# Hedgehog attention with a gated MLP: two heads' output rows moved into spare rows, and another order of loads and stores in the output stage

## The chip, the cores and the metric

The kernel runs on one core of a Trainium2 chip. A core has five engines that work side by side: TensorE (PE, matrix products, with its weight loads shown as PEld), VectorE (DVE), ScalarE (ACT), GpSimd (POOL) and SyncE (SP), which here does little but issue DMAs. The metric is the device time in microseconds (us) of one execution; the number compared is the median of several executions. The kernel before takes 686.28 us (three runs, 686.24 to 686.62).

## The reference

With S = 2048 tokens, D = 640, 32 heads of 20 columns, F = 1536, all in float32:

```python
qkv = (x @ wqkv)                      # split in q, k, v and 32 heads
pq, pk = q @ w_phi, k @ w_phi         # per head, 20 x 20
phi_q = concat(softmax(pq), softmax(-pq))   # 40 features a head
phi_k = concat(softmax(pk), softmax(-pk))
kv, z = phi_k^T @ v, sum_s phi_k      # per head, 40 x 20 and 40
o = (phi_q @ kv) / (phi_q . z + 1e-6)
s = o @ wo                            # heads side by side, 640 x 640
g = silu(gelu(xn @ w1 + b1) @ w2 + b2)
out = x + s * g                       # xn = layernorm(x) feeds both branches
```

## The kernel before, in words

The kernel has three stages. The first (0 to about 270 us) normalises x, projects keys, values and queries, and sums `kv` and `z` over all tokens. The second (to about 580 us) is the MLP, in twelve units; beside it the query features are normalised tile by tile (`q_norm`, 128 tokens a tile) and written to a DRAM array `phi_dram`. The third is the output stage, to which nearly all of the change belongs.

Matrix products keep float32 accuracy by splitting each operand in a high and a low part (type `F32R`) and adding three products: high times high, high times low, low times high (`PASSES`).

**The output stage.** Tokens are handled in four chunks of 512 (`ORDER` = chunks 2, 3, 0, 1; the loop index is `ci`), each in five *blocks* `d`, one for each 128 output columns. A block is one pass of the inner loop:

- `load_res` loads the residual x (`xres`) and, for the first two chunks, the gate (`gt`) of the block two further on;
- `finish(c, d, ...)` multiplies the chunk's attention output `oT` with `wo` in 16 matmuls, multiplies with the gate (VectorE), adds the residual (GpSimd) and stores 256 KB;
- `num_groups` takes a quarter of the work on the next chunk's attention output. There are twelve steps `(j, p)`: `j` is a group of six heads (j = 5 the last two heads, 30 and 31) and `p` a half of the chunk (two tiles of 128 tokens). `num_t` transposes the features `phi` of a step on TensorE and copies them to `ph`; a block later `num_m` multiplies them with the block-diagonal `bdk` (or `bdl` for j = 5), and ScalarE and VectorE write the result's high and low part into `oT`;
- `late_q` carries on the normalisation of the last four query tiles (4 to 7): `q_load` loads one (`eq`, 640 KB), GpSimd and VectorE work on it, and it is stored to `phi_dram`. This runs through the first chunk and the first two blocks of the second.

An attention output of six heads has 120 rows; `bdk` spaces it to 2 x 64 rows, so that 8 of the 128 rows of each of the five `oT` tiles are zero, and `wo` is laid out to match (680 rows). The last two heads' 40 rows stand three times in a tile of their own, `oTl` (high, low and high part), and the sixteenth matmul of `finish` multiplies it with `wol`, which `load_wol` prepares (40 rows of `wo` three times).

`load_phi(c)` issues the loads of a chunk's four `phi` tiles (640 KB each) together: for the third chunk in block 0 of `ci` 0, for the fourth in block 3 of `ci` 1.

**What sets the order.** Everything here stands under `manual_schedule`, so each engine executes its instructions in the order in which the Python code issues them. SP issues every load and store of this stage, in that same order; an instruction that waits holds all that SP has behind it. Tiles come from pools of fixed size (`slabs` 23, `rows` 11, `late` 13); a tile that is asked for when all are taken waits until an older one is read for the last time.

Of the kernel before, what the change touches and what calls it, by code (L numbers as in the profile page):

```python
# [45 lines left out]
def hedgehog_gated_mlp_kernel(ctx: ExitStack, tc: tile.TileContext, x, xt_in, wqk, bd, wv, wo, w1, b1, w2, b2, out_t):  # L46
# [62 lines left out]
    for h in range(3):  # L109
# [4 lines left out]
    lowsel = const.tile([P, 1], F32, name="lowsel")  # L114
    nc.gpsimd.memset(lowsel[:], -1.0)
    nc.gpsimd.affine_select(out=lowsel[:], in_=lowsel[:], pattern=[[0, 1]],
                            compare_op=OP.is_ge, fill=0.0, base=-80, channel_multiplier=1)
    midsel = const.tile([P, 1], F32, name="midsel")
    nc.gpsimd.memset(midsel[:], -1.0)
    nc.gpsimd.affine_select(out=midsel[:], in_=midsel[:], pattern=[[0, 1]],  # L120
                            compare_op=OP.is_ge, fill=0.0, base=-40, channel_multiplier=1)
    nc.gpsimd.affine_select(out=midsel[:], in_=midsel[:], pattern=[[0, 1]],
                            compare_op=OP.is_ge, fill=0.0, base=79, channel_multiplier=-1)
    const.tile([P, 8], F32, name="align")
    bdk = const.tile([P, 10, 64], F32, name="bdk")
    bdl = const.tile([P, 120], F32, name="bdl")
# [436 lines left out]
    def kv_rest():  # L563
        kv_acc(NT - 1, phis.pop(NT - 1), vs.pop(NT - 1))
        kvr = const.tile([P, 360], F32, name="kvr")
        nc.gpsimd.memset(kvr[64:96, 320:360], 0.0)
        nc.gpsimd.memset(kvr[96:, 240:360], 0.0)
        for p, a, b in ((P, 0, 240), (96, 240, 320), (64, 320, 360)):
            nc.scalar.activation(kvr[:p, a:b], kvp[0][:p, a:b], AF.Copy)
        return kvr  # L570


    def kv_state(kvr):
        nc.gpsimd.memset(bdk[:, :, 60:], 0.0)
# [4 lines left out]
        nc.vector.tensor_tensor(bdk[:120, :, :60].rearrange("p f (h d) -> p f h d", d=20),  # L579
                                s3[:, :, None, :20].to_broadcast([120, 10, 3, 20]),  # L580
                                mask[:120, None, :, None].to_broadcast([120, 10, 3, 20]), op=OP.mult)
        for r in range(3):
            nc.vector.tensor_tensor(bdl[:80, 40 * r:40 * r + 40].rearrange("p (h d) -> p h d", d=20),
                                    ps[:80, None, 320:340].to_broadcast([80, 2, 20]),
                                    mask[:80, :2, None].to_broadcast([80, 2, 20]), op=OP.mult)
# [95 lines left out]

    def q_load(t):
        e = slab(F32, "eq")
        ef = e[:].rearrange("p a b -> p (a b)")
        nc.sync.dma_start(ef, e_dram[t])
        return ef

    def q_norm(t, ef):
        ez = slab(F32, "ez")
        zv = ez[:].rearrange("p a b -> p (a b)")  # L690
        nc.gpsimd.tensor_tensor(zv, ef, zf, op=OP.mult)  # L691
# [12 lines left out]
        nc.vector.tensor_tensor(r3, r3, den[:, :, None].to_broadcast([P, 32, 2]), op=OP.mult)  # L704
        yield
        scale_heads(ef, rc)
        yield
        nc.sync.dma_start(phi_dram[t], ef)

    def load_wol():  # L710
        raw = row([P, D], F32, "raw")
        for r in range(3):
            nc.sync.dma_start(raw[40 * r:40 * r + 40, :], wo[640:680, :])
        wol_h = row([P, D], F32R, "wolh")
        wol = row([P, D], F32R, "wol")
        nc.vector.tensor_copy(wol_h[:120, :], raw[:120, :])
        nc.vector.scalar_tensor_tensor(wol[:120, :], wol_h[:120, :].bitcast(F32), midsel[:120, :], raw[:120, :],
                                       op0=OP.mult, op1=OP.add)
        return wol


    def load_phi(c):
        tl = [slab(F32R, "phi", (P, 2 * D)) for _ in range(TPC)]
        for i in range(TPC):
            nc.sync.dma_start(tl[i][:].bitcast(F32), phi_dram[TPC * c + i])
        return tl
# [14 lines left out]
    def num_m(j, oT, p, n, ph):  # L741
# [9 lines left out]
        else:  # L751
            for a, b in ((0, 64), (64, 120)):
                nc.tensor.matmul(po[a:b, :256], bdl[:n, a:b], ph[:n, :256], start=True, stop=True)  # L753
            o2 = oT[1]
            nc.scalar.activation(o2[:120, 0, sl], po[:120, :256], AF.Copy)
            nc.vector.scalar_tensor_tensor(o2[:120, 1, sl], o2[:120, 0, sl].bitcast(F32), lowsel[:120, :],
                                           po[:120, :256], op0=OP.mult, op1=OP.add)

    def num_groups(phi, oT, size=4):
        steps = [(j, p) for p in range(2) for j in range(6)]  # L760
        before = []
        for k in range(0, 12, size):
            now = [(j, p, *num_t(phi, p, j)) for j, p in steps[k:k + size]]
            for j, p, n, ph in before:
                num_m(j, oT, p, n, ph)
            before = now
            yield
        for j, p, n, ph in before:
            num_m(j, oT, p, n, ph)
# [29 lines left out]
    def finish(c, d, oT, last):  # L799
        ps = bankB()  # L800
        steps = [(wo_s[j][:, b, d * P:(d + 1) * P], oT[0][j][:, a, :]) for j in range(5) for a, b in PASSES]
        steps.append((wol[:120, d * P:(d + 1) * P], oT[1][:120, 1, :]))
        for n, (w, o) in enumerate(steps):
            nc.tensor.matmul(ps[:], w, o, start=n == 0, stop=n == 15)  # L804
        xr, gt = xres.pop((c, d)), gates.pop((c, d))
        for o in range(2):
            sl = slice(o * W2, (o + 1) * W2)
# [3 lines left out]
            if last:  # L811
                nc.sync.dma_start(out_t[d * P:(d + 1) * P, c * CW + o * W2:c * CW + (o + 1) * W2], xr[:, sl])
        if not last:
            nc.sync.dma_start(out_t[d * P:(d + 1) * P, c * CW:(c + 1) * CW], xr[:])
# [138 lines left out]
    wol = load_wol()  # L953
# [28 lines left out]
    lq = late_q()  # L982
    for ci, c in enumerate(ORDER):
        nxt = iter(())
# [3 lines left out]
        for d in range(KC):  # L988
            load_res(ci * KC + d + 2)
# [14 lines left out]
def _layout(A_x, A_wqkv, A_w_phi, A_wo, B_w1, B_b1, B_w2, B_b2):  # L1004
# [5 lines left out]
    wo = np.zeros((680, D), a["wo"].dtype)  # L1010
    for k in range(10):
        wo[64 * k:64 * k + 60] = a["wo"][60 * k:60 * k + 60]
    wo[640:] = a["wo"][600:]
# [37 lines left out]
```

## Time and profile before

| what | value |
|---|---|
| median of three runs | 686.28 us (686.24 to 686.62) |
| the profiled execution | 688.63 us |
| its span, first to last instruction | 686.9 us |
| PE busy | 676.7 us (99%), 4713 matmul records |
| DVE, ACT, POOL busy | 455.5, 251.3, 375.6 us |
| L804 (`finish`) with `oT` and `wo` | 300 records, 72.9 us |
| L804 with `oTl` and `wol` | 20 records |
| DMA | 125.73 MB, mean 183 GB/s |

Times in a row are counted from the span's start. A row of the timeline has the start, the length (of all merged instructions), the engine, the line of the kernel, the operation, the tiles (written <- read), the shape and the count. A matmul's own length (about 390 ns) is that of its way through the pipeline; how long one holds TensorE is seen from the distance of two starts. A row of windows has the stretch, the busy time of PE, PEld, DVE, ACT and POOL in it (with counts), the granted TensorE clock, the DMA engines' busy share and GB/s.

### The profile page before, as it was taken

The page shows a single profiled execution, that of the slowest core. Times are in us where ns is not written, and L with a number is a line of the kernel's source. Part 1 is how long each engine was busy: PE and PEld are TensorE (multiplying, and loading weights), DVE is VectorE, ACT ScalarE, POOL GpSimd, SP SyncE. Part 2 cuts the span into 40 slices and gives each one's busy share as a digit, 9 for nine tenths or more (in the row PEclk, how much of TensorE's full clock was granted, in tenths as well). Part 3 has the DMA queues.
Part 4 walks back from the last instruction along what each step waited for, and adds up shares of the span by engine and source line. Part 5 has one row for each costly group of instructions (what it writes and reads, how often), then busy time and mean ns, then how long its engine had stood idle before and what let it go on. Part 6 is the DMA issues. An engine that isn't in the chain of part 4 may idle for free.

```text
span 686.9 us, 11941 instructions
## 1 busy us (share of the span) xinstructions
PE 676.7 (99%) x4713; PEld 590.6 (86%) x4713; DVE 455.5 (66%) x730; ACT 251.3 (37%) x398; POOL 375.6 (55%) x336
## 2 busy tenths in 40 slices
PE   8899999999999999999999999999999999999997
PEld 8899999999999998888887888888888887777875
DVE  4788566886876456677978774676977655774232
ACT  3332313323332237244353347633233354425430
POOL 1355244859577355866968853636456640783221
PEclk9999999999999999999999999999999999999999
DMA  9820052734261153329687697376364491886623
GB/s 339 305 88 2 3 150 81 242 79 149 51 216 59 80 171 134 115 70 329 211 301 260 210 421 319 90 266 240 140 206 153 145 396 49 314 295 210 231 93 107
DMA packets 73966, 125.73 MB, mean 183 GB/s; under 512 B 5694, under 2 KB 42558, under 8 KB 73014
## 3 DMA queue, kind: packets, MB, share of 16 engines
q1 hardware_dynamic: 71606, 114.48, 48.9%
q10 hardware_dynamic: 2304, 10.49, 4.2%
q8 instruction: 37, 0.61, 0.4%
q14 instruction: 19, 0.16, 0.1%
HBM read 79.85 MB, written 45.10 MB: 182 GB/s over the span
## 4 chain that ended last, share of the span: by engine, by line
PE 90%; DVE 5%; ACT 1%; issue 1%; DMA 1%; POOL 1%; SPq 0%; DVEq 0%; POOLq 0%; ACTq 0%
PE pA L306 30%; PE pB L645 22%; PE pB L616 18%; PE pB L804 11%; PE pB L746 3%; PE pB L735 2%; PE kv L377 2%; PE pA L163 2%; DVE y L654 2%; DVE xhi L670 1%; DMA xt<-in_x_dram 1%; PE pA L292 1%; PE pB L753 1%; DVE rc L340 0%; PE pB L590 0%
## 5 line engine op out<-in xcount | busy, mean ns | idle before, releaser
L645 PE MATMUL pB<-hs,w2s 128*128 128x512 f32 x720 | 167.1, 390 | 0.0
L645 PEld LDWEIGHTS pB<-hs,w2s 128*128 128x128 f32 x720 | 134.7, 188 | 29.2 <-PE pB L746 0.8
L616 PE MATMUL pB<-xp,w1s 128*128 128x512 f32 x324 | 81.4, 390 | 1.0 <-DVE pB L888 1.0
L616 PE MATMUL pB<-xd,w1s 128*128 128x512 f32 x324 | 79.3, 389 | 0.0
L332 ACT ACTIVATE e<-e 128x1280 f32<-128x1280 f32 x32 | 40.7, 1272 | 91.5 <-POOL e L327 91.0
L804 PE MATMUL pB<-oT,wo 128*128 128x512 f32 x300 | 72.9, 394 | 0.0
L616 PEld LDWEIGHTS pB<-xp,w1s 128*128 128x128 f32 x324 | 60.7, 188 | 13.9 <-DVE pB L888 1.4
L654 DVE TENSOR_TENSOR y<-pB,y 128x512 f32<-128x512 f32 x100 | 63.9, 680 | 12.3 <-PE pB L645 12.1
L616 PEld LDWEIGHTS pB<-xd,w1s 128*128 128x128 f32 x324 | 60.8, 188 | 12.6
L804 PEld LDWEIGHTS pB<-oT,wo 128*128 128x128 f32 x300 | 55.4, 188 | 14.8 <-ACT ph L738 1.2
L345 POOL TENSOR_TENSOR e<-e,rc 128x1280 f32<-128x1280 f32 x16 | 39.0, 2440 | 48.5 <-DVE rc L365 48.2
L345 POOL TENSOR_TENSOR eq<-eq,rc 128x1280 f32<-128x1280 f32 x16 | 38.0, 2372 | 50.0 <-DVE rc L704 50.0
L327 POOL TENSOR_TENSOR e<-nr,e 128x640 f32<-128x640 f32 x32 | 45.4, 1421 | 33.5 <-DVE nr L326 30.7
L306 PE MATMUL pA<-wv,xp 128*128 128x320 f32 x384 | 61.0, 312 | 0.8 <-DVE nr L326 0.4
L621 ACT ACTIVATE pB<-pB,b1t 128x512 f32<-128x512 f32 x48 | 31.8, 662 | 77.3 <-DVE pB L888 28.4
L306 PE MATMUL pA<-wk,xp 128*128 128x320 f32 x384 | 59.9, 311 | 0.0
L306 PE MATMUL pA<-wq,xp 128*128 128x320 f32 x384 | 59.0, 309 | 0.0
L306 PEld LDWEIGHTS pA<-wv,xp 128*128 128x128 f32 x384 | 56.9, 188 | 1.7 <-issue 0.7
L306 PEld LDWEIGHTS pA<-wq,xp 128*128 128x128 f32 x384 | 56.9, 188 | 0.1
L306 PEld LDWEIGHTS pA<-wk,xp 128*128 128x128 f32 x384 | 56.8, 188 | 0.1
L691 POOL TENSOR_TENSOR ez<-eq,zrep 128x1280 f32<-128x1280 f32 x16 | 47.3, 2953 | 1.1 <-PE pB L753 1.1
L401 POOL TENSOR_TENSOR w1s<-raw,w1s 128x640 fp32r<-128x640 f32 (+1 forms) x18 | 25.7, 1429 | 36.8 <-ACT w1s L400 29.6
(139 smaller groups left out, 1046.0 us busy)
## 6 DMA issues: line engine op xcount, KB each, us to landing
raw<-in_w_dram SPq DMA_DIRECT2D x42, 320.0 KB, 4.4
e_dram<-e ACTq DMA_DIRECT2D x16, 640.0 KB, 3.3
eq<-e_dram SPq DMA_DIRECT2D x16, 640.0 KB, 6.9
phi_dram<-eq SPq DMA_DIRECT2D x16, 640.0 KB, 3.4
phi<-phi_dram SPq DMA_DIRECT2D x16, 640.0 KB, 9.5
xt<-in_x_dram SPq DMA_DIRECT2D x16, 320.0 KB, 4.8
xres<-in_xt_dram SPq DMA_DIRECT2D x20, 256.0 KB, 4.5
out_dram<-xres SPq DMA_DIRECT2D x18, 256.0 KB, 3.0
```

The lines of the kernel that those rows point to most:

```text
L306: nc.tensor.matmul(ps[:, hf, :HALF], stat_x(q, o, k, a), ws[k][:, b, hf * HALF:(hf + 1) * HALF], start=n == 0, stop=n == 3 * KC - 1)
L327: nc.gpsimd.tensor_tensor(e5[:, :, :, 1, :], nr[:, :, :, None].to_broadcast([P, 2, 16, DH]), e5[:, :, :, 0, :], op=OP.subtract)
L332: nc.scalar.activation(ef, ef, AF.Exp)
L345: nc.gpsimd.tensor_tensor(e3, e3, rc[:, :, None].to_broadcast([P, 64, DH]), op=OP.mult)
L401: nc.gpsimd.tensor_tensor(sl[:, 1, :n], src, sl[:, 0, :n].bitcast(F32), op=OP.subtract)
L616: nc.tensor.matmul(bank[ch][:], tl[:, a, off + wo_:off + wo_ + P], mov(blk, b), start=new and n == 0, stop=n == len(mms) - 1, skip_group_c ...
L621: nc.scalar.activation(ps, ps, AF.Gelu_apprx_tanh, bias=b1t[:, f:f + 1])
L645: nc.tensor.matmul(ps[:], ws[i][:, b, d * P:(d + 1) * P], hs[o][i][:, a, :], start=i == n == 0, stop=(i, n) == (GF - 1, 2), skip_group_che ...
L654: nc.vector.tensor_tensor(y, ps[:], y, op=OP.add)
L691: nc.gpsimd.tensor_tensor(zv, ef, zf, op=OP.mult)
L746: nc.tensor.matmul(po[64 * e:64 * e + 64, :256], bdk[:n, 2 * j + e, :], ph[:n, e * 256:(e + 1) * 256], start=True, stop=True)
L804: nc.tensor.matmul(ps[:], w, o, start=n == 0, stop=n == 15)
```

## The change

- The 40 rows of heads 30 and 31 are computed once, not three times: `bdl` shrinks to 40 columns and `num_m` for j = 5 needs one matmul, writing high and low part into rows 0 to 39 of `oT[1]`.
- `bdk` is laid out so that every sixteenth row of an `oT` tile is free (rows 15, 31, ..., 127: 8 rows), built in `kv_state` by three VectorE operations, one a head. `spread(j, oT)` copies rows 8j to 8j+7 of `oT[1]` there by a DMA from SBUF to SBUF (32 KB), issued by SP when both halves of group j are done. `wo` is laid out to match and shrinks to 640 rows.
- So the sixteenth matmul of `finish`, `load_wol` and the constants `lowsel` and `midsel` go.
- `num_groups` takes the steps group by group, j = 5 first, both halves after each other.
- `load_phi_tile` loads one `phi` tile a block: in `ci` 0 in blocks 0 to 3; in `ci` 1 two in block 1 and one each in blocks 2 and 3.
- In the output stage the stores of `finish` and of `late_q` are put in a list (`put`) and issued in the next block (`put_old`), after that block's spreads and ahead of its `phi` load; in the last chunk at the end of the same block.

```diff
-        for r in range(3):
-            nc.vector.tensor_tensor(bdl[:80, 40 * r:40 * r + 40].rearrange("p (h d) -> p h d", d=20),
...
+        for h in range(3):
+            nc.vector.tensor_scalar(
+                bdk[:120].rearrange("p f (q c) -> p f q c", c=16)[:, :, :, 5 * h:5 * h + 5],
+                s3[:, :, :20].rearrange("p f (q i) -> p f q i", i=5), mask[:120, h:h + 1], None, op0=OP.mult)
+        nc.vector.tensor_tensor(bdl[:80].rearrange("p (h d) -> p h d", d=20),
...
+    stores, late_store = [], [False]
+
+    def put(dst, src):
+        if late_store[0]:
+            stores.append((dst, src))
+        else:
+            nc.sync.dma_start(dst, src)
+
+    def put_old(n):
+        for _ in range(n):
+            nc.sync.dma_start(*stores.pop(0))
...
-        nc.sync.dma_start(phi_dram[t], ef)
+        put(phi_dram[t], ef)
...
+    def load_phi_tile(c, i):
+        t = slab(F32R, "phi", (P, 2 * D))
+        nc.sync.dma_start(t[:].bitcast(F32), phi_dram[TPC * c + i])
+        return t
...
-            for a, b in ((0, 64), (64, 120)):
-                nc.tensor.matmul(po[a:b, :256], bdl[:n, a:b], ph[:n, :256], start=True, stop=True)
+            nc.tensor.matmul(po[:40, :256], bdl[:n, :], ph[:n, :256], start=True, stop=True)
...
+    def spread(j, oT):
+        nc.sync.dma_start(oT[0][j][15::16].bitcast(F32), oT[1][8 * j:8 * j + 8].bitcast(F32))
 
     def num_groups(phi, oT, size=4):
-        steps = [(j, p) for p in range(2) for j in range(6)]
+        steps = [(j, p) for j in (5, 0, 1, 2, 3, 4) for p in range(2)]
         before = []
+
+        def products(group):
+            for j, p, n, ph in group:
+                num_m(j, oT, p, n, ph)
+                if p and j < 5:
+                    spread(j, oT)
...
-        steps.append((wol[:120, d * P:(d + 1) * P], oT[1][:120, 1, :]))
         for n, (w, o) in enumerate(steps):
-            nc.tensor.matmul(ps[:], w, o, start=n == 0, stop=n == 15)
+            nc.tensor.matmul(ps[:], w, o, start=n == 0, stop=n == 14)
...
+    late_store[0] = True
     for ci, c in enumerate(ORDER):
-        nxt = iter(())
+        nxt, phi2 = iter(()), []
         if ci + 1 < NCH:
             oTn = new_oT(late if ci % 2 else slabs)
             nxt = num_groups(phin, oTn)
         for d in range(KC):
+            old = len(stores)
             load_res(ci * KC + d + 2)
             finish(c, d, oT, ci == NCH - 1 and d >= 3)
             next(lq, None)
...
             next(nxt, None)
-            if ci + 2 < NCH and d == (0 if ci == 0 else 3):
-                phin = load_phi(ORDER[ci + 2])
+            put_old(old if ci + 1 < NCH else len(stores))
+            if ci + 2 < NCH and d >= ci:
+                while len(phi2) < min(TPC, d + 1):
+                    phi2.append(load_phi_tile(ORDER[ci + 2], len(phi2)))
             next(lq, None)
         if ci + 1 < NCH:
-            oT = oTn
+            oT, phin = oTn, phi2
```

More of the change, by code (lines that the diff above doesn't have):

```diff
@@ L113, in hedgehog_gated_mlp_kernel @@
                                 compare_op=OP.is_ge, fill=0.0, base=40 * h + 39, channel_multiplier=-1)
[L114 to L124, printed above, removed]
+    const.tile([P, 24], F32, name="align")
     bdk = const.tile([P, 10, 64], F32, name="bdk")
-    bdl = const.tile([P, 120], F32, name="bdl")
+    bdl = const.tile([P, 40], F32, name="bdl")
     def load_x(t):
@@ L564, in kv_rest @@
         kv_acc(NT - 1, phis.pop(NT - 1), vs.pop(NT - 1))
-        kvr = const.tile([P, 360], F32, name="kvr")
+        kvr = const.tile([P, 376], F32, name="kvr")
         nc.gpsimd.memset(kvr[64:96, 320:360], 0.0)
@@ L573, in kv_state @@
     def kv_state(kvr):
-        nc.gpsimd.memset(bdk[:, :, 60:], 0.0)
+        nc.gpsimd.memset(bdk[:, :, 15::16], 0.0)
         ps = bankB()
@@ L707, in q_norm @@
         yield
-        nc.sync.dma_start(phi_dram[t], ef)
[L710 to L719, printed above, removed]
-    def load_phi(c):
[L723 to L726, printed above, removed]
+        put(phi_dram[t], ef)
+    def load_phi(c):
+        return [load_phi_tile(c, i) for i in range(TPC)]
+    def load_phi_tile(c, i):
+        t = slab(F32R, "phi", (P, 2 * D))
+        nc.sync.dma_start(t[:].bitcast(F32), phi_dram[TPC * c + i])
+        return t
     def num_t(phi, p, j):
@@ L811, in finish @@
             if last:
[L812 removed]
+                nc.sync.dma_start(out_t[d * P:(d + 1) * P, c * CW + o:c * CW + o + W2], xr[:, sl])
         if not last:
[L814 removed]
+            put(out_t[d * P:(d + 1) * P, c * CW:(c + 1) * CW], xr[:])
     zf, none = None, iter(())
@@ L1009, in _layout @@
     bd = np.zeros((P, 6, 120), a["wphi"].dtype)
[L1010 to L1013, printed above, removed]
+    wo = np.zeros((D, D), a["wo"].dtype)
+    w4 = wo.reshape(10, 4, 16, D)
+    w4[:, :, :15] = a["wo"][:600].reshape(10, 3, 4, 5, D).transpose(0, 2, 1, 3, 4).reshape(10, 4, 15, D)
+    w4[:, :, 15] = a["wo"][600:].reshape(10, 4, D)
     for h in range(H):
```

23 lines of the change are left out of this document (8 added, 15 removed).

## The prediction

> **What bounds the kernel now.** I read the page first (busy time, chain), then the TensorE timeline of the last 110 us, where all of the change's matmuls lie, then the queue of SyncE (SP) and the DMA throughput there.
>
> ```profile
> PE 676.7 (99%) x4713; PEld 590.6 (86%) x4713; DVE 455.5 (66%) x730; ACT 251.3 (37%) x398; POOL 375.6 (55%) x336
> PE 90%; DVE 5%; ACT 1%; issue 1%; DMA 1%; POOL 1%; SPq 0%; DVEq 0%; POOLq 0%; ACTq 0%
> ```
>
> TensorE (PE) works through the span and 90% of the chain is PE, so a matmul less is worth its spacing wherever nothing makes PE wait. The rows of PE at the start of the output stage (start, length, line, tiles, count; chunk index `ci` 0):
>
> ```profile
> 579.52 3.56 PE L804 MATMUL pB<-oT,wo 128*128 128x512 f32 x15
> 582.92 0.39 PE L804 MATMUL pB<-oTl,wol 120*128 120x512 f32 x1
> 583.15 1.43 PE L735 MATMUL pB<-identr,phi 128*120 128x128 f32 x16
> 584.42 3.67 PE L804 MATMUL pB<-oT,wo 128*128 128x512 f32 x15
> ...
> 596.11 0.65 PE L746 MATMUL pB<-ph,bdk 120*64 120x256 f32 x4
> 596.59 0.60 PE L753 MATMUL pB<-ph,bdl 80*64 80x256 f32 x4
> 597.02 1.03 PE L746 MATMUL pB<-ph,bdk 120*64 120x256 f32 x8
> 597.99 3.70 PE L804 MATMUL pB<-oT,wo 128*128 128x512 f32 x15
> ...
> 607.49 3.58 PE L804 MATMUL pB<-oT,wo 128*128 128x512 f32 x15
> 610.91 0.40 PE L804 MATMUL pB<-oTl,wol 120*128 120x512 f32 x1
> 611.15 1.43 PE L735 MATMUL pB<-identr,phi 128*120 128x128 f32 x16
> ```
>
> PE has no hole here: a block is `finish` (16 matmuls), then transposes (L735) and products (L746, L753) for the next chunk. The first 15 start over 582.92-579.52 = 3.40 us, 0.227 each; the sixteenth, of `wol`, takes 583.15-582.92 = 0.23.
>
> What feeds this stage is nearly full. SP's queue, then DMA throughput in four windows (last column GB/s):
>
> ```profile
> 585.32 0.34 SPq L814 DMA_DIRECT2D out_dram<-xres  x1
> 585.75 0.38 SPq L685 DMA_DIRECT2D eq<-e_dram  x1
> 586.19 2.30 SPq L725 DMA_DIRECT2D phi<-phi_dram  x4
> ```
>
> ```profile
> 579.00:582.00 3.00, 3.00 (x14) 2.46 (x14) 0.74 (x2) 0.00 (x0) 0.00 (x0) 1.00 0.00 0
> 591.00:594.00 3.00, 3.00 (x16) 2.35 (x13) 3.00 (x7) 0.78 (x3) 3.00 (x2) 1.00 1.01 418
> 585.00:606.00 21.00, 21.00 (x133) 15.72 (x132) 15.04 (x31) 8.39 (x22) 15.68 (x10) 1.00 0.94 340
> 593.00:606.00 13.00, 13.00 (x82) 9.54 (x81) 9.35 (x18) 4.58 (x12) 10.48 (x8) 1.00 1.00 386
> ```
>
> Before, the four `phi` tiles that are wanted at 611.15 are issued together at 586.19, 25 us ahead. That margin is what the change spends.
>
> **The change part by part.**
>
> *The sixteenth matmul of `finish`.* 20 calls (4 chunks x 5) x 0.23 = **-4.6 us**, all on PE.
>
> *The product of heads 30 and 31.* Two matmuls of 64 and 56 columns become one of 40, in 8 steps. The step of four records now takes 597.02-596.59 = 0.43, like a step of L746 ((597.99-597.02)/2 = 0.48).
>
> ```profile
> 596.58:596.70 0.12, 0.11 (x2) 0.11 (x2) 1.00 1.02 401
> ```
>
> Two records lie in that 0.12 us, so the column halves run side by side and half of the records cost no time of their own. If they ran in turn, 8 x 0.21 = 1.7 us would go; I take 0, and 0 to -1.7 as bounds.
>
> *`kv_state`, constants, `wol`.* VectorE (DVE) now spends one 773 ns and three 185 ns operations in `kv_state`; three of a third of the width each and one of 185 come to 0.3 us either side of that. GpSimd's constants at 1.5 to 2.8 us go, beside PE's warm-up. The two `wol` operations on DVE go, beside PE's stream.
>
> ```profile
> L579 DVE TENSOR_TENSOR bdk<-pB,mask x1: 773/773/773, 432.6 to 432.6; 120x600 f32<-120x600 f32 x1
> L583 DVE TENSOR_TENSOR bdl<-pB,mask x3: 185/185/185, 433.3 to 433.5; 80x40 f32<-80x40 f32 x3
> L717 DVE SCALAR_TENSOR_TENSOR wol<-wolh,midsel,raw x1: 1970/1970/1970, 565.9 to 565.9; 120x640 fp32r<-120x640 f32 x1
> ```
>
> All are covered by PE's matmuls: 0 (without that cover, 0.3 us either way).
>
> *The spreads.* Five DMAs of 32 KB a chunk copy 8 rows of heads 30 and 31 into row 15, 31, ... of each `oT` tile; the next `finish` reads them. No row shows such a transfer. The nearest are the stores:
>
> ```profile
> out_dram<-xres SPq DMA_DIRECT2D x18, 256.0 KB, 3.0
> out_dram<-xres SPq DMA_DIRECT2D x4, 128.0 KB, 1.9
> ```
>
> On an idle queue I take 1.9 us (smaller still, so nearer the 128 KB row; bounds 1.9 and 3.0). Before the first chunk the last subtraction ends about 578.8, so the fifth spread lands by 580.7 to 581.8; its first reader is matmul 13, at 579.5+12x0.227 = 582.2: no wait. But each spread is issued by SP, waits there for DVE, and holds what is queued behind it.
>
> *Stores a block later, `phi` a tile a block.* SP's standstill now is the store, behind GpSimd:
>
> ```profile
> SPq L814 <- POOL xres L810: 67.3, 17, 14.8
> ```
>
> That wait goes. In `ci` 0 the new order is: block 0 two loads for block 2, `eq` 5, `phi` tile 0; block 1 two loads, spread 0, store 0, `phi` tile 1, `eq` 6; block 2 two loads, spreads 1 and 2, store 1, `phi` store 4, `phi` tile 2; block 3 two loads, `eq` 7, spreads 3 and 4, store 2, `phi` store 5, `phi` tile 3. Spread 0 waits for the fourth subtraction of block 1, spread 2 for that of block 2. Their places are in DVE's and GpSimd's rows, whose order the change keeps:
>
> ```profile
> 585.25 2.94 POOL L691 TENSOR_TENSOR ez<-eq,zrep 128x1280 f32<-128x1280 f32 x1
> 588.23 1.49 DVE L340 TENSOR_REDUCE dn<-ez 128x64 f32<-128x1280 f32 x1 [2.14 <-POOL ez L691]
> 590.62 0.23 DVE L704 TENSOR_TENSOR rc<-rc,den 128x64 f32<-128x64 f32 x1
> 591.43 1.41 DVE L750 TENSOR_TENSOR oT<-pB,oT 128x256 fp32r<-128x256 f32 x4
> ...
> 594.71 2.92 POOL L691 TENSOR_TENSOR ez<-eq,zrep 128x1280 f32<-128x1280 f32 x1
> 597.67 1.49 DVE L340 TENSOR_REDUCE dn<-ez 128x64 f32<-128x1280 f32 x1 [1.75 <-POOL ez L691]
> 600.94 0.74 DVE L750 TENSOR_TENSOR oT<-pB,oT 128x256 fp32r<-128x256 f32 x2
> ```
>
> The subtractions end at 592.84 and 601.68, less the 0.2 that `finish` 0 is shorter. So SP stands from about 585 to 592.6 with the DMA engines running dry, and what follows must then go through one queue: stores 0 to 2 and the two loads each of blocks 2 and 3 (7 x 256 KB), `phi` tiles 1 to 3, `eq` 6 and 7, `phi` stores 4 and 5 (7 x 640), five spreads (160): 6,432 KB, 6.59 MB. At 340 GB/s, the row that begins like this burst from an idle queue, that is 19.4 us: 612.0. The first 2,048 KB (store 0, tile 1, `eq` 6, two loads; 6.2 us) are through at 598.8, and the next stand behind spread 2 until 601.5: 2.7 us idle, so `phi` tile 3 is there at **614.7**. Bounds: 15.8 us at 418 GB/s without a pause, 608.4; and 614.7 with the 1.9 us of a landing on top, 616.6.
>
> When is it wanted? The new step order takes heads 30 and 31 first, for both halves of the chunk, so the second pair of transposes already reads tiles 2 and 3. They stand at 611.15 less six removed matmuls, 609.8 (+0.1). PE therefore waits 614.7-609.9 = **+4.8 us** (0 to 6.7). Inside it lies a wait of `finish` for spread 3, behind `eq` 7 in the queue: wanted after nine matmuls, at 607.49-5x0.23+9x0.227 = 608.4; there 1,536 KB (4.6 us) ahead of tile 3, at 610.1.
>
> By the Trainium skill (DMA: Bandwidth & Descriptors, section Specifications), the fabric's ceiling is 435 GB/s and the HBM limit of one core about 358 GB/s. By the first, 6.59 MB would take 15.1 us (an estimate) and the wait would vanish; by the second, 18.4 us; the trace's windows lie between 340 and 418.
>
> *The next boundary (`ci` 1 to 2).* No `eq` and one `phi` store are left, so the queue clears. The last tile is issued some 2.1 us after the last product (subtraction, spread, store), and a single load lands 5.5 us after its issue:
>
> ```profile
> DMA to landing us min/median/max: 5.5/5.5/5.5
>   DMA phi<-phi_dram: 0.3, 1
> ```
>
> 7.6 us against two `finish` calls of 15 (6.8) and a pair of transposes, 7.0: 0.6 of waiting, where PE waits 0.3 now (second row): **+0.3** (0 to +0.6). `ci` 2 to 3 has no `phi` load: 0.
>
> *Sum.* -4.6 + 4.8 + 0.3 = **+0.5 us**. The profiled execution took 688.63 us (span 686.9), so it would take 689.1; the median shown is 686.28, 2.35 lower, and the forecast for it **686.8**.
>
> **Rivals.**
>
> *Transfers hidden* (faster): the queue runs near the 418 of its best window and DVE releases the spreads sooner. With a wait of 0 to 1.5 us: 681.7 to 683.5. For it: 386 over 13 us once the queue is full. Against it: the idle stretch before 592.6 is set by DVE and GpSimd, which the change does not touch.
>
> *The clock gate* (slower). PE's clock fell when it stood still at the end (its last matmul starts at 681.7 and takes 0.395; the granted clock is the third column from the right of the windows):
>
> ```profile
> L804 PE MATMUL pB<-oTl,wol x20: 391/395/402, 582.9 to 681.7; 120*128 120x512 f32 x20
> ...
> 682.20:685.60 3.40, 0.00 (x0) 0.00 (x0) 1.61 (x4) 0.00 (x0) 0.00 (x0) 1.00 0.22 77
> 685.00:686.00 1.00, 0.00 (x0) 0.00 (x0) 0.00 (x0) 0.00 (x0) 0.00 (x0) 0.79 0.15 50
> 686.00:687.00 1.00, 0.00 (x0) 0.00 (x0) 0.00 (x0) 0.00 (x0) 0.00 (x0) 0.50 0.00 0
> ```
>
> Full until 3.4 us after it, then half. My wait comes in two pieces, 610.1-608.4 = 1.7 us for spread 3 and 4.8-1.7 = 3.1 for tile 3, with six matmuls between. From 3.4 us in one piece, 0.3 more than I forecast, the clock can fall: at half clock over as long again, 1.7 us are lost, 688.5 to 690 with the longer wait. The Trainium skill (TensorE: Matmul & The Clock Gate, section Part 1: The HAM clock gate) gives an idle window of about 3.4 us and half rate after it; the trace agrees (1.00 to 0.50 after 3.4 us).
>
> *A second jam* (slower): the load of the last tile of chunk 1 also waits for its own store, issued a block before; if the first jam pushes that back by another 640 KB (1.9 us at 340 GB/s), PE stands that much longer at `ci` 1 to 2: 688.7.
>
> **How the numbers follow.** One jam 0.50, around 686.8, own range 685.3 to 688.3; hidden 0.30; clock gate 0.13; second jam 0.07. A measurement tells 0.2% (1.4 us) from no change: under 684.9 is faster, over 687.7 slower. The jam's half falls 0.04 / 0.28 / 0.18 on the three, so faster 0.34, same 0.28, slower 0.38. The range leaves out the best of the hidden cases and the worst of the gate: 682.2 to 689.8.
>
> **What would show it.** L804 with 300 records and none of `wol`; SP standing at the spreads for DVE; `phi` tile 3 landing some 5 us after the transposes are due, as idle time of L735 put down to a DMA at `ci` 0 to 1; idle time of L804 put down to `oT` just before. Without that idle time I am wrong and the kernel gains over 3 us; with PE's clock below 1.00 in that stretch the gate has spoken.

## The result, and the profile after

The changed kernel takes **692.8 us** (median, 691.96 to 694.0) against 686.39 us (686.24 to 686.62) measured beside it: a ratio of 1.0094, 95% interval 1.0077 to 1.0112. It is 6.4 us slower. The forecast was 686.8 us with a range of 682.2 to 689.8, so the time lies outside it, on the side of the clock gate rival and beyond what that rival was given. Two executions among the experiments, which ran at a granted clock of 0.85 and 0.75 throughout, are left out of every number below.

Line numbers moved: `finish` multiplies in L802 (L804 before), `num_t` transposes in L728 (L735), a `phi` tile is loaded in L718, a spread is issued in L751, an old store in L683. The page of the changed kernel, its busy times, its chain and the group of `finish`:

```profile
PE 674.0 (98%) x4677; PEld 588.1 (85%) x4677; DVE 450.8 (65%) x728; ACT 251.4 (36%) x398; POOL 375.9 (54%) x331
PE 86%; DVE 5%; DMA 5%; POOL 2%; issue 1%; ACT 1%; SPq 1%; DVEq 0%; POOLq 0%; ACTq 0%
L802 PE MATMUL pB<-oT,wo 128*128 128x512 f32 x300 | 74.2, 403 | 4.2 <-DMA oT<-oTl 4.2
```

TensorE has fewer instructions and is busy for less time, yet its share of the chain fell from 90% to 86% and that of DMA rose from 1% to 5%. `finish` has its 300 records and none of `wol`, and it now stands idle for a spread (`oT<-oTl`). All that TensorE waits for in the output stage, by the view of waits (total, times, longest, in us):

```profile
PE pB L802 <- DMA oT<-oTl: 4.2, 1, 4.2
PE pB L728 <- DMA phi<-phi_dram: 3.1, 2, 2.2
```

These are 7.3 us; before, the same view lists no wait of PE in this stage. Where they lie is seen in the timeline of TensorE, from the last block of the first chunk on; the last nine matmuls of the first row and what follows answer to the rows from 607.49 on of the kernel before:

```profile
602.82 3.33 PE L802 MATMUL pB<-oT,wo 128*128 128x512 f32 x14
610.33 2.90 PE L802 MATMUL pB<-oT,wo 128*128 128x512 f32 x6 [4.18 <-DMA oT<-oTl]
613.03 0.53 PE L728 MATMUL pB<-identr,phi 128*80 128x128 f32 x3
615.74 1.29 PE L728 MATMUL pB<-identr,phi 128*80 128x128 f32 x9 [2.18 <-DMA phi<-phi_dram]
616.83 3.40 PE L802 MATMUL pB<-oT,wo 128*128 128x512 f32 x9
```

The first `finish` of the second chunk does nine matmuls, stands 4.18 us for spread 3, does the other six, and then the transposes of the second pair stand 2.18 us for `phi` tile 3. Two more things are in these rows: the six matmuls from 610.33 on take 2.90 us, and nine from 616.83 on take 3.40, where 15 took 3.56 before. TensorE runs at half speed there. The windows (third column from the right: the granted clock; last: GB/s) show it:

```profile
605.60:608.90 3.30, 0.56 (x3) 0.13 (x1) 1.83 (x5) 0.00 (x0) 2.46 (x3) 1.00 0.98 368
609.00:619.20 10.20, 6.68 (x24) 5.30 (x25) 5.18 (x9) 1.85 (x4) 7.72 (x5) 0.50 1.03 380
619.30:625.00 5.70, 5.70 (x40) 4.33 (x40) 1.41 (x4) 3.02 (x8) 1.42 (x2) 1.00 0.24 94
590.90:615.70 24.80, 18.48 (x101) 13.47 (x99) 17.96 (x34) 5.20 (x13) 20.39 (x15) 0.86 0.88 297
```

The fourth row is the jam, from the first store after spread 0 to the transposes that read `phi` tile 3; the DMA engines are 0.88 busy in it. What SP did meanwhile:

```profile
582.79 0.32 SPq L787 DMA_DIRECT2D gt<-g_dram  x1
590.34 0.58 SPq L751 DMA_DIRECT2D oT<-oTl  x1
590.97 0.43 SPq L683 DMA_DIRECT2D out_dram<-xres  x1
...
598.46 1.27 SPq L751 DMA_DIRECT2D oT<-oTl  x2
...
603.40 1.25 SPq L751 DMA_DIRECT2D oT<-oTl  x2
...
606.90 0.32 SPq L718 DMA_DIRECT2D phi<-phi_dram  x1
607.55 0.33 SPq L783 DMA_DIRECT2D xres<-in_xt_dram  x1
608.30 0.39 SPq L787 DMA_DIRECT2D gt<-g_dram  x1
610.02 0.34 SPq L683 DMA_DIRECT2D out_dram<-xres  x1
```

SP issues nothing for 590.34-582.79 = 7.6 us, standing at spread 0. Its largest wait in the output stage is now for the subtraction that writes `oT`:

```profile
SPq L751 <- DVE oT L743: 61.9, 14, 11.2
```

The wait for GpSimd at the store (67.3 us before, 17 times) has been exchanged for one for VectorE at the spread (61.9 us, 14 times).

**Where the 6 us are.** The output stage, from the first to the last matmul of `finish`, ran from 579.5 to 681.7 before (102.2 us). After:

```profile
L802 PE MATMUL pB<-oT,wo x300: 387/389/767, 577.2 to 685.1; 128*128 128x512 f32 x150
```

That is 107.9 us, 5.7 more. The profiled executions differ by less (691.96 against 688.63) because the one of before reached this stage 2.3 us later than the one of after (579.5 against 577.2; the profiles below start it at 577.0 to 578.4). So stages are compared below, not profiled totals.

### The profile page after: what moved, and what is told of

Read it like the earlier page. It is cut to its first block, busy times and chain, and to the rows that moved or that the text cites. A ratio compares the mean times of both kernels' runs of the same rounds, so it can differ in the third digit from the quotient of the medians.

```text
span 690.2 us, 11903 instructions
## 1 busy us (share of the span) xinstructions
PE 674.0 (98%) x4677; PEld 588.1 (85%) x4677; DVE 450.8 (65%) x728; ACT 251.4 (36%) x398; POOL 375.9 (54%) x331
## 4 chain that ended last, share of the span: by engine, by line
PE 86%; DVE 5%; DMA 5%; POOL 2%; issue 1%; ACT 1%; SPq 1%; DVEq 0%; POOLq 0%; ACTq 0%
PE pA L296 30%; PE pB L636 22%; PE pB L607 19%; PE pB L802 7%; DMA phi<-phi_dram 3%; PE pB L739 2%; PE pA L153 2%; PE kv L367 2%; PE pB L728 2%; DVE y L645 1%; POOL ez L694 1%; DMA folds<-in_wqk_dram 1%; DMA w_dram<-w1s 1%; DVE dn L330 1%; PE pA L282 1%
## 5 line engine op out<-in xcount | busy, mean ns | idle before, releaser
L802 PE MATMUL pB<-oT,wo 128*128 128x512 f32 x300 | 74.2, 403 | 4.2 <-DMA oT<-oTl 4.2
L802 PEld LDWEIGHTS pB<-oT,wo 128*128 128x128 f32 x300 | 56.9, 193 | 19.5 <-issue 5.0
```

The source lines that it names most:

```text
L802: nc.tensor.matmul(ps[:], w, o, start=n == 0, stop=n == 14)
```

## The experiments

Two theories stand against each other. **A**: all of the loss is waiting of TensorE for late transfers, and what the clock loses after such a wait. **B**: something else in the change costs time too (the order of the work, the layout with its spare rows, the spreads as such). Within A it has to be told what makes the transfers late: the spreads that SP waits at, or the `phi` tiles that are issued late.

**The sixteenth matmul alone** (kernel before without it and without `wol`):

```diff
-        steps.append((wol[:120, d * P:(d + 1) * P], oT[1][:120, 1, :]))
-            nc.tensor.matmul(ps[:], w, o, start=n == 0, stop=n == 15)
+            nc.tensor.matmul(ps[:], w, o, start=n == 0, stop=n == 14)
-    wol = load_wol()
```

> The kernel before without the sixteenth matmul of finish and without wol (heads 30 and 31 are left out of the result): the price of the removed matmuls alone. Theory (TensorE sets the pace, 0.23 us a matmul): 686.4 - 20 x 0.23 = 681.8, and no wait of TensorE. Rival (other engines, VectorE's subtractions above all, are next behind it and take part of the gain): 683.5 or more, with idle time of L804 put down to DVE or DMA.

Measured 682.68 us, ratio 0.9946 (0.9928 to 0.9964). Its stage:

```profile
L803 PE MATMUL pB<-oT,wo x300: 387/389/504, 577.7 to 675.4; 128*128 128x512 f32 x150
```

97.7 us, 4.5 less than before (the medians, 682.68 and 686.55 beside it, differ by 3.9): the gain that was forecast at 4.6 is real, and nearly all of it is paid where nothing else interferes.

**The order alone** (kernel before with the change's step order, late stores and single `phi` loads; no spreads, sixteenth matmul and `wol` kept):

```diff
-        steps = [(j, p) for p in range(2) for j in range(6)]
+        steps = [(j, p) for j in (5, 0, 1, 2, 3, 4) for p in range(2)]
-            nc.sync.dma_start(out_t[d * P:(d + 1) * P, c * CW:(c + 1) * CW], xr[:])
+            put(out_t[d * P:(d + 1) * P, c * CW:(c + 1) * CW], xr[:])
-            if ci + 2 < NCH and d == (0 if ci == 0 else 3):
-                phin = load_phi(ORDER[ci + 2])
+            put_old(old if ci + 1 < NCH else len(stores))
+            if ci + 2 < NCH and d >= ci:
+                while len(phi2) < min(TPC, d + 1):
+                    phi2.append(load_phi_tile(ORDER[ci + 2], len(phi2)))
```

> The kernel before with the change's order alone: one phi tile a block, stores one block later, steps group by group; no spreads, the sixteenth matmul and wol kept. Theory (the late tile is a cost of its own, as in the run without spreads, where tile 3 landed 2.2 us after it was due; here it is due 6 x 0.23 = 1.4 us later): a wait of about 1 us for a phi tile at ci 0 to 1, about 687.3. Rival (order is harmless without spreads): 686.5 or less.

Measured 687.11 us, 1.0007 (0.9997 to 1.0016): no difference from before. Its stage runs from 577.3 to 679.3, 102.0 us. The wait of about 1 us for a `phi` tile that was expected did not come: TensorE waits for no DMA in the stage; its one wait of the stage, and the DMA throughput in the stretch that jams in the changed kernel:

```profile
PE pB L760 <- DVE oTl L770: 0.3, 1, 0.3
```

```profile
595.00:612.00 17.00, 17.00 (x94) 13.03 (x91) 14.31 (x28) 4.96 (x14) 13.58 (x11) 1.00 0.98 355
```

TensorE is busy for all of the 17.00 us. In this kernel, which has no spreads and keeps the sixteenth matmul, the order and the late loads cost nothing.

**No spreads** (changed kernel without them):

```diff
-                if p and j < 5:
-                    spread(j, oT)
```

> The changed kernel without the spreads: the output of heads 30 and 31 is left out of the result; everything else, the phi loads and late stores too, stays. Theory (the standstill of SyncE at the spreads and the spreads' place in the queue make the jam): SyncE issues its loads as soon as tiles are free, no wait of finish, no wait for phi tile 3, no half clock, and the last boundary's 0.9 us goes: 692.8 - 4.2 - 2.2 - 3.2 - 0.9 = about 682.3. Rival (one phi tile a block is too late by itself, with or without spreads): the transposes still wait 2 us or more for phi tile 3 and the time stays over 685.

Measured 683.2 us, 0.995 (0.9931 to 0.9969), where 682.3 and no wait were expected. Its one wait for a DMA in the stage:

```profile
PE pB L728 <- DMA phi<-phi_dram: 2.2, 1, 2.2
```

So the late tile is a cost of its own, also without spreads. Why the kernel before with the order alone had no such wait is shown only in part. The six sixteenth matmuls make the same transposes due 6 x 0.23 = 1.4 us later, which is less than 2.2; and by the packets of the two traces tile 3 took 7.4 us from its issue to its last packet there (600.93 to 608.36) and 8.8 us here (601.52 to 610.29). What made it slower here stays open. The clock stayed at 1.00 through this wait of 2.2 us:

```profile
606.70:610.00 3.30, 1.85 (x11) 1.35 (x9) 3.16 (x7) 0.38 (x1) 2.46 (x3) 1.00 1.03 395
610.10:613.40 3.30, 2.65 (x18) 2.33 (x19) 0.59 (x2) 1.41 (x3) 3.30 (x2) 1.00 0.99 370
```

**Spreads alone** (changed kernel with stores at once, all `phi` loads together as before, and the halves one after the other):

```diff
-    late_store[0] = True
-        steps = [(j, p) for j in (5, 0, 1, 2, 3, 4) for p in range(2)]
+        steps = [(j, p) for p in range(2) for j in (5, 0, 1, 2, 3, 4)]
-            put_old(old if ci + 1 < NCH else len(stores))
-            if ci + 2 < NCH and d >= ci:
-                while len(phi2) < min(TPC, d + 1):
-                    phi2.append(load_phi_tile(ORDER[ci + 2], len(phi2)))
+            if ci + 2 < NCH and d == (0 if ci == 0 else 3):
+                phi2 = load_phi(ORDER[ci + 2])
```

> The changed kernel's arithmetic alone: spreads and no sixteenth matmul, but stores at once, phi tiles loaded together as before, and the steps half by half (heads 30 and 31 first in each half, so that the spreads can follow). Theory (SyncE stands at a store for GpSimd with the last spreads behind it): finish waits 2 to 3 us for a spread at each of the three boundaries, 686.5 - 4.4 + 3 x 2 to 3 = 688 to 691. Rival (only the late tiles are at fault): no such wait, about 682.5.

Measured 692.1 us, 1.0086 (1.0063 to 1.0108), as slow as the change and 1.1 us over the upper end expected. The expected 2 to 3 us at each of three boundaries did not come; instead one wait of 6.0 us for a spread stands at the first boundary, longer than that of the change. Below the waits stand SP's waits for GpSimd at a store between 590 and 612 us, and SP's queue:

```profile
PE pB L802 <- DMA oT<-oTl: 6.0, 1, 6.0
PE pB L728 <- DMA phi<-phi_dram: 1.5, 2, 1.2
```

```profile
SPq L679 <- POOL xres L808: 9.0, 3, 5.0
```

```profile
605.55 0.34 SPq L679 DMA_DIRECT2D out_dram<-xres  x1
605.94 0.42 SPq L688 DMA_DIRECT2D eq<-e_dram  x1
606.46 2.56 SPq L751 DMA_DIRECT2D oT<-oTl  x4
```

SP issues four spreads in a row, the first at 606.46, after TensorE has begun to wait (605.1), because they stand behind a store that waits for GpSimd. So the loss does not need the other order and the late stores: with the old ones the last spreads come later still (606.46 against 603.40 in the change).

**Early `phi`** (changed kernel, all four tiles of the first chunk's successor issued in block 0):

```diff
-            if ci + 2 < NCH and d >= ci:
+            if ci == 0 and d == 0:
+                phi2 = load_phi(ORDER[2])
+            if ci == 1 and d >= 1:
```

> The changed kernel, but in the first chunk (ci 0) all four phi tiles are loaded together in block 0, as before the change; ci 1 unchanged. Theory (late loads jam the DMA queue: phi tile 2 stands in the queue ahead of spread 3, and phi tile 3 behind it): the wait of the transposes for phi tile 3 at ci 0 to 1 (2.2 us in the changed kernel) goes, the wait of finish for spread 3 (4.2 us) shortens by the 640 KB of tile 2 at 340 GB/s, 1.9 us, to about 2.3 us, too short for TensorE's clock to fall, so the half-clock stretch (some 3.2 us lost) goes too: 692.8 - 2.2 - 1.9 - 3.2 = about 685.5. Rival (a spread is slow by itself, or TensorE waits for VectorE whatever is loaded when): the 4.2 us wait and the half clock stay, 690 or more.

Measured 687.92 us, 1.0015 (1.0001 to 1.0029). The wait for the tiles at the first boundary is gone, the one for spread 3 stays at 2.19 us, as expected; what was not expected is the clock, which fell after a wait of 2.19 us:

```profile
608.33 2.46 PE L802 MATMUL pB<-oT,wo 128*128 128x512 f32 x6 [2.19 <-DMA oT<-oTl]
```

```profile
605.50:608.80 3.30, 1.11 (x5) 0.65 (x4) 1.90 (x5) 0.00 (x0) 2.46 (x3) 1.00 1.02 375
608.90:612.20 3.30, 3.30 (x18) 2.77 (x17) 2.55 (x4) 1.08 (x3) 3.30 (x2) 0.50 1.00 339
```

**Spreads a block later** (changed kernel, spreads 0 to 2 issued at the head of the next block, behind its two loads and ahead of the old stores, when VectorE is long done):

```diff
-                    spread(j, oT)
+                    if late_store[0] and j < 3:
+                        wait_spread.append((j, oT))
+                    else:
+                        spread(j, oT)
...
             load_res(ci * KC + d + 2)
+            while wait_spread:
+                spread(*wait_spread.pop(0))
```

> The changed kernel with spreads 0 to 2 issued one block later, phi tiles still one a block: only SyncE's standstill in blocks 1 and 2 is taken away. Theory (the standstill lets the DMA engines run dry and what follows then stands ahead of spread 3): the wait for spread 3 at ci 0 to 1 falls from 4.2 us to 1 us or less; phi tile 3 is still issued behind spread 4 in block 3 and lands some 7 us after, a wait of 2 to 3.5 us for it stays: 684 to 685.5. Rival (late tiles alone are the cause): as the changed kernel, 690 or more.

Measured 687.43 us, 1.0012 (1.0001 to 1.0023), 1.9 us over the upper end expected. The wait for a spread is gone and the one for `phi` tile 3 has doubled, although its transposes start sooner than in the change (612.39 against 615.74 in the timelines): with no wait for a spread ahead of them they are due sooner too.

```profile
PE pB L728 <- DMA phi<-phi_dram: 5.0, 2, 4.4
```

```profile
607.70:611.00 3.30, 0.30 (x4) 0.14 (x2) 2.71 (x5) 0.38 (x1) 3.00 (x2) 1.00 0.88 266
611.20:617.90 6.70, 5.51 (x20) 4.55 (x21) 2.48 (x5) 1.47 (x3) 5.28 (x4) 0.50 1.03 395
```

**Both repairs** (early `phi` and later spreads, all in the first chunk):

> The two repairs of the first chunk only: all four phi tiles of its successor loaded in block 0, spreads 0 to 2 a block later; the second chunk's loads stay as the change has them. Theory (two separate waits in the first chunk, each with its own remedy, and a boundary after the second chunk that costs about 1 us): 681.5 to 682.5 us, no wait for a spread or a phi tile near 605 to 616 us, clock 1.00, a wait of 0.3 to 1.2 us near 638 to 644. Rival (the early loads push spread 3 back, as they were seen to keep a wait of 2.2 us for it, so that the deferral does not help): 685 us or more, with the wait for spread 3 still there.

Measured 682.37 us, 0.9938 (0.9921 to 0.9955). One wait is left in the stage, at the second boundary:

```profile
PE pB L728 <- DMA phi<-phi_dram: 0.3, 1, 0.3
```

The two waits are separate, and each has its own remedy; in the executions that were profiled, either remedy alone left a wait long enough for the clock to fall.

**The second chunk too** (as before, and in `ci` 1 the tiles are issued in blocks 0 (two), 2 and 3, ahead of the old stores):

```diff
+            if ci == 0 and d == 0:
+                phi2 = load_phi(ORDER[2])
+            if ci == 1 and d in (0, 2, 3):
+                while len(phi2) < (2 if d == 0 else d + 1):
+                    phi2.append(load_phi_tile(ORDER[3], len(phi2)))
             put_old(old if ci + 1 < NCH else len(stores))
```

> The changed kernel with three things undone or eased: all four phi tiles of the third chunk are loaded in block 0 of ci 0; in ci 1 the tiles are loaded in blocks 0 (two), 2 and 3, ahead of the old stores; and spreads 0 to 2 are issued one block later, when their data has long been ready, so that SyncE stands only at spreads 3 and 4. Theory (late tiles and SyncE's standstill together make the jam): no wait of finish for a spread and none of the transposes for a tile beyond 0.5 us, no half clock, and the whole price of the sixteenth matmul is kept: 686.5 - 4.4 = about 682.2, at most 683.2. Rival (a spread takes too long even in a clear queue): idle time of L802 put down to oT<-oTl stays over 1 us, 684 or more.

Measured 680.88 us (the middle of three), 0.992 (0.9903 to 0.9936). The same kernel again, with its profile:

> The kernel of early and deferred transfers once more, for a profile of its output stage. Theory (waits and the clock are all that the change cost, and both are gone here): 681 us, TensorE without an idle piece above 0.5 us between 600 and 650 us, the granted clock 1.00 throughout the output stage, and that stage, first finish matmul to last, 98 us (102.2 before less 4.4). Rival (a cost of the spreads other than waiting, for instance slower SBUF access of the matmuls while they run): the stage at 99 us or more with no such piece.

Measured 681.18 us, 0.992 (0.9905 to 0.9935). TensorE waits for no DMA in the stage, and:

```profile
577.00:678.00 101.00, 97.53 (x565) 76.11 (x563) 48.13 (x109) 36.34 (x83) 46.51 (x44) 1.00 0.65 223
```

```profile
L805 PE MATMUL pB<-oT,wo x300: 388/389/499, 577.0 to 674.1; 128*128 128x512 f32 x150
```

The clock is 1.00 throughout and the stage 97.1 us, 5.1 under before (98 was expected). This is the change's whole gain with all its waits taken away, and it is 5.3 us (0.8%) faster than the kernel before and 11.6 us faster than the change as it was made. The order of the steps, the late stores, the layout and the spreads are all in this kernel, so theory B has nothing left to explain.

**The clock by itself** (changed kernel, with 18 more matmuls at the head of the second chunk's first `finish`, which its first matmul overwrites):

```diff
+        if (c, d) == (ORDER[1], 0):
+            for _ in range(18):
+                nc.tensor.matmul(ps[:], wo_s[0][:, 0, :P], oT[0][0][:, 0, :], start=True, stop=True)
```

> The changed kernel with 18 extra matmuls of 0.227 us (4.1 us, into the same PSUM bank, overwritten after) ahead of finish in block 0 of the second chunk, where TensorE stands for spread 3: its standstill is filled with work of the same length. Theory (the standstill lets TensorE's clock fall to half for some 10 us, which costs some 3.2 us by itself): the granted clock stays at 1.00 there, and the time falls by about 3 us, to 689.5. Rival (the half clock costs nothing because TensorE waits for phi tile 3 anyway): no change or up to 4 us slower, 692.5 to 697.

Measured 1.0076 (1.005 to 1.0102), which does not stand clear of the change's 1.0094 (1.0077 to 1.0112). The same kernel again, with its profile:

> The kernel with 18 extra matmuls once more, for a profile of the stretch in which the clock fell. The extra matmuls stand at the head of the second chunk's first block, are overwritten by the first matmul of finish, and take 18 x 0.23 = 4.1 us, about the length of the wait for spread 3. Theory (the clock falls because TensorE is mostly idle over one of its windows): with the first wait filled, the clock stays at 1.00 until the wait for phi tile 3, which is 2 to 4 us long and either lies across two windows (clock 1.00 throughout, time 690 us) or fills one (half clock for one or two windows after it, time 691.5 us). Rival (the clock falls with the jam of the DMAs itself, not with an idle TensorE): half clock near 609 us although TensorE is busy there, and 692.8 us.

Measured 692.67 us, 1.0086 (1.0069 to 1.0103), 1.2 us over the 691.5 expected for one or two windows at half clock, so the time alone does not decide between the two. The timeline and the windows of TensorE:

```profile
605.14 4.24 PE L803 MATMUL pB<-oT,wo 128*128 128x512 f32 x18
609.22 2.20 PE L805 MATMUL pB<-oT,wo 128*128 128x512 f32 x9
612.70 1.63 PE L805 MATMUL pB<-oT,wo 128*128 128x512 f32 x6 [1.28 <-DMA oT<-oTl]
...
617.10 1.07 PE L728 MATMUL pB<-identr,phi 128*80 128x128 f32 x9 [2.60 <-DMA phi<-phi_dram]
```

```profile
605.00:611.00 6.00, 6.00 (x28) 4.98 (x27) 3.62 (x7) 0.00 (x0) 4.62 (x5) 1.00 0.99 337
614.20:617.60 3.40, 0.81 (x10) 0.65 (x9) 2.94 (x6) 0.52 (x2) 2.80 (x3) 1.00 1.02 384
617.70:621.00 3.30, 3.30 (x11) 2.71 (x11) 0.56 (x2) 1.17 (x3) 2.36 (x1) 0.50 1.03 408
```

With TensorE busy the clock stays up although the DMA engines are as full as in the change (0.99), and it falls only after the later wait, for one window. So an idle TensorE brings the clock down, and the jam does not. As a price of the clock the run is no use: the added 4.1 us cancel what is saved.

**The account.** For each kernel: the waits for DMA in the output stage by the view of waits, half of TensorE's busy time in the stretch at clock 0.50 (by which that work is longer than at full clock), the 5.1 us gained without waits, and the sum beside the stage's measured change against 102.2 us.

| kernel | waits | half clock | sum | measured |
|---|---|---|---|---|
| the change | 7.3 | 6.68/2 = 3.3 | +5.5 | +5.7 |
| spreads alone | 7.5 | 4.85/2 = 2.4 | +4.8 | +5.5 |
| 18 more matmuls (+4.1) | 6.2 | 3.30/2 = 1.7 | +6.9 | +7.6 |
| spreads a block later | 5.0 | 5.51/2 = 2.8 | +2.7 | +2.8 |
| early `phi` | 3.1 | 3.30/2 = 1.7 | -0.3 | +0.2 |
| no spreads | 2.2 | 0 | -2.9 | -2.6 |
| both repairs, first chunk | 0.3 | 0 | -4.8 | -4.6 |
| the second chunk too | 0 | 0 | -5.1 | -5.1 |

The last row is so by definition. The others close to within 0.8 us, and the remainder is always on the slow side; small pieces that no view puts down to a DMA must make it up, and were not traced.

Two things limit the table. Waits and half clock add up, but they are not two separate prices: where work at half clock stands ahead of a wait, that work at full clock would have ended sooner and waited longer for the same transfer. And each row is one execution: that of early `phi` lies 1.5 us under its kernel's median (686.38 against 687.92), that of spreads a block later 1.8 us over (689.24 against 687.43). Of the ten executions of the latter, four had a granted clock of 0.994 and took 687.8 to 689.2 us, the other six had 0.996 to 0.998 and took 685.9 to 688.6.

## Why the prediction was wrong

The structure was right and the sum was not. The steps, in the prediction's terms:

- *The sixteenth matmul*, -4.6: right (-4.5 alone). *The product of heads 30 and 31, `kv_state`, constants*, 0: right, or nearly. The stage without waits gained 5.1, and the starts of the matmuls in the traces tell where: from first to last start the 20 calls of `finish` take 69.7 us in all before and 64.9 there, 4.7 less. Another 0.2 us was a small hole before, at the boundary of `ci` 1 to 2: the block there took 5.11 us against 4.90 and 4.92 at the same place in the other chunks. The 0.1 to 0.2 us that is left is all that the product can have given; the bound of -1.7 was far off. (The 0.3 us that the prediction reads at that boundary as a wait of PE is in the list of waits a row of the weight load, PEld.)
- *A spread on an idle queue*, 1.9 us: right. Spread 0 was issued at 590.34, and its packets ran from 591.56 to 592.36, 2.0 us after the issue.
- *SP stands at spread 0 and the DMA engines run dry*: right to the tenth. Spread 0 was forecast for 592.6; the stage begins 2.3 us earlier in the profile of after, which makes it 590.3 on that axis, and 590.34 was measured. The two waits also came in the forecast order and at the forecast instructions.
- *Then 6.59 MB go through one queue*, tile 3 there at 614.7, or 612.4 on the axis of after: **this step failed.** The transposes that wait for tile 3 started at 615.74, 3.3 us later. The mean rate was not the fault: 22.1 us for 6.59 MB is 298 GB/s, and the window from the first store to these transposes shows 297. What was wrong is what I had let go through and where I had let it begin and end. The packets of the trace can be told apart by size: 5,120 bytes are rows of `phi` and `eq`, 4,096 of a spread, 2,048 of a residual, a gate or a store. From the issue of spread 0 up to tile 3's last packet, which ended at 615.26, the seven transfers of 640 KB and the five spreads are there as counted, but 1,157 packets of 2,048 bytes instead of 7 x 128 = 896. The 261 more, 0.53 MB or 1.8 us at 297 GB/s, are by their order the two loads issued right behind tile 3 (607.55 and 608.30) and the first rows of the store after them: the packets of these loads start from 612.80 to 615.13, beside those of tile 3, which start from 611.97 to 615.06. I had let the queue end with the tile; what is issued behind it takes its share of the DMA engines before the tile is complete. The rest are two delays that I had put at nothing: 1.2 us from the issue of spread 0 to its first packet, and 0.5 us from tile 3's last packet to the transposes. The Trainium skill (DMA: Bandwidth & Descriptors, section Queues, rings and completion order) says that each DMA engine takes its own ring in order, but that completion is not first in, first out for an issuing engine, which fits.
- *Spread 3*, 1.7 us inside the tile's wait: measured 4.2. It was issued at 603.40 and let TensorE go at 610.33, 6.9 us later. The forecast for its arrival was 610.1-2.3 = 607.8, so it was 2.5 us late. Here no bytes were missing from the sum: the packets of spreads 3 and 4 start from 609.02 to 609.59, ahead of those of the two loads behind tile 3. The same two delays were missing: 1.2 us ahead of the first packet of the jam, and 0.6 to 0.9 us from the end of the spread's packets to TensorE's start (those of spreads 3 and 4 are mixed and end from 609.18 to 609.75). The 0.4 to 0.7 us that is left stays open.
- *The clock gate*, a rival at 0.13 that was to need 3.4 us of idle time in one piece: **the second failed step.** It fell after 2.8 us of idle time (the nine matmuls' end at about 606.2 to 609.0), and in the kernel with early `phi` after 2.2. The half clock stretched the work by 3.3 us, twice the 1.7 given, because the rest of the first wait kept it down for a second window and the second wait for a third. But half of that was no loss by itself. Tile 3 was issued at 606.90, before the clock fell; the work between the two waits (610.33 to 613.56) would at full clock have ended 1.6 us sooner and waited 1.6 us longer for the tile. What the clock added to the time is the work from 615.74 to 619.21, 3.5 us at half clock, so about 1.7. This is an estimate from the rows; no run holds the clock up with the rest unchanged.
- *The next boundary*, +0.3: measured 0.9 (3.1-2.2).

So the forecast of 0.5 = -4.6 + 4.8 + 0.3 stands against 5.5 = -5.1 + 6.4 + 3.3 + 0.9 by the rows of waits and clock. By cause, the 4.8 were 8.1: the transposes were due at 609.9-2.3 = 607.6 and started at 615.74. Some 1.6 us of that delay were filled with work at half clock and so do not show as waiting. With the 1.7 us that the clock cost after it, the sum is -5.1 + 8.1 + 1.7 + 0.9 = 5.6, and 5.7 was measured. Of the 5.1 us between forecast and sum, 3.3 are tile 3, 1.7 the clock, 0.6 the second boundary, less 0.5 of gain. The upper bound of 6.7 us for the first delay was too low, and the range had nothing for the clock on top of it.

Of the rivals, hidden transfers and the second jam are refuted by the waits of the changed kernel (6.4 us at the first boundary, 0.9 at the second, against 1.9 us more that the second jam asked for). The signs that were named for the forecast itself were there: no records of `wol`, SP at the spreads, idle time of the transposes put down to a DMA, idle time of `finish` put down to `oT`, and, for the gate, the clock below 1.00. Only the size differed: tile 3 was 8.1 us late for the transposes, where some 5 had been named.

## What to carry to other kernels

A small transfer that the issuing engine must wait for is dear by what stands behind it in the queue: place it where its source has long been written, and put the loads with a due time ahead of it. When a forecast counts on bytes ahead of a deadline, count also those issued right behind it (here two transfers of 256 KB), the time to the first packet and the time from the last packet to the reader. And price a wait of a saturated TensorE with the clock: here a window of 3.4 us full of work took 1.7 us longer at half clock, which is lost where no later wait would have taken that time anyway.

## What the runs showed of the hardware

The clock changes on a grid. In the trace's clock records (start, length, clock), every length from the first one at 1.00 on, but for the last, which the end cuts off, is a whole number of 3.413 us (in brackets):

```
the change          4.81  604.16 (177)  1.00;  10.24 (3)  0.50;  68.27 (20)  1.00
early phi           4.68  604.16 (177)  1.00;   3.41 (1)  0.50;  71.68 (21)  1.00
spreads later       6.95  604.16 (177)  1.00;   6.83 (2)  0.50;  68.27 (20)  1.00
18 more matmuls     6.62  610.99 (179)  1.00;   3.41 (1)  0.50;  71.68 (21)  1.00
no spreads          5.92  675.84 (198)  1.00
```

So what counts is the share of such a window in which TensorE stands. Early `phi`: the window up to 608.84 held 2.19 us of waiting, 64%, and the clock fell for the next. The change: 82% idle up to 608.97. No spreads: the same 2.2 us lay across two windows (1.85 of 3.30 us and 2.65 of 3.30 us busy in the rows above; by the trace 1.53 and 0.67 us of the 3.41 idle, 45% and 20%), and nothing fell. Between 45% and 64% lies the limit in these runs; none tells it closer. The clock came back only after a window with no wait in it: in the change the window from 608.97 to 612.39 was busy from 610.33 on, so 40% idle, and did not bring it back. The Trainium skill (TensorE: Matmul & The Clock Gate, section Part 1: The HAM clock gate) speaks of a free-running window of 4096 cycles and of half rate after an idle one of about 3.4 us. The grid agrees; that the window must be idle as a whole does not: 64% was enough.
